# Another table of planner rules: which of sixteen rule sets orders each stretch of a two-layer transformer kernel

## The chip, the cores and the metric

The kernel runs on one core of one Trainium2 chip. The engines are TensorE (PE, with its weight loads as PEld), VectorE (DVE), ScalarE (ACT), GpSimd (POOL) and SyncE (SP, which issues the DMAs). The metric is the device time of one execution in microseconds, less being better. Each time is a median over several executions.

## The reference

Two attention blocks and two MLP blocks alternate over 2048 tokens of width 512, each behind a layer norm without weights and each with a residual. Both layers use the same weights. The attention has 32 heads of 16 columns; the MLP has 1792 hidden columns and a tanh GELU.

```python
def _A_ref(x, wqkv, wo):
    qkv = (x @ wqkv).reshape(B, S, 3, H, Dh)          # S = 2048, H = 32, Dh = 16
    q, k, v = ...                                     # each (B, H, S, Dh)
    scores = jnp.einsum("bhqd,bhkd->bhqk", q, k) * (Dh ** -0.5)
    p = _softmax(scores, axis=-1)
    o = jnp.einsum("bhqk,bhkd->bhqd", p, v)
    return o.transpose(0, 2, 1, 3).reshape(B, S, D) @ wo

def _B_ref(x, w1, b1, w2, b2):
    return _gelu(x @ w1 + b1) @ w2 + b2               # 512 -> 1792 -> 512

x = A_x
x = x + _A_ref(_layernorm(x), A_wqkv, A_wo)
x = x + _B_ref(_layernorm(x), B_w1, B_b1, B_w2, B_b2)
x = x + _A_ref(_layernorm(x), A_wqkv, A_wo)
return x + _B_ref(_layernorm(x), B_w1, B_b1, B_w2, B_b2)
```

All inputs are bfloat16. `B_x` isn't used.

## The kernel before, in words

**The work.** The unit of attention is a cell: one key tile of 128 keys, one group `a` of 32 of the 128 partitions (two heads), and 512 columns, which are 256 or 512 queries of those heads. There are 4096 cells over both layers. For each cell PE computes scores into one PSUM bank (`score`, L1444), an engine takes the exponential out of the bank, and PE multiplies the result with 17 columns of V, the 17th being ones for the softmax's sum (`pvs`, L2009). The banks: ACT's two slots hold banks 0, 1 and 3, 4 (`SLOTS`), with banks 2 and 5 lendable as a third to either slot (`THIRD`); bank 6 collects the products with V (`PVB`); bank 7 and, at times, 5 serve the projections and the MLP (`MISC`).

**Two ways to an exp.** ACT takes two or three cells with one instruction (`exps`, L1943), 128x1024 or 128x1536. DVE takes one cell with one instruction (`dfirst`, L1625), which writes a 16-bit integer that, read as bfloat16, is an approximate exponential; POOL adds constants to such a row three times over for shifted copies (`dchain`, L1717), and PE multiplies the four copies of a cell with V and three weighted copies of V (`VC`), so that a DVE cell has four matmuls with V where an ACT cell has one. Only the cells of five of the sixteen key tiles of each layer (`KD`, L54) may go to DVE. What of these DVE has not taken when ACT's own list for a head group is empty, ACT takes (`next_act`).

**Beside the attention** go, tile by tile: layer norms (`ln`, DVE, with a transposing DMA), the projections to Q, K, V (`proj`), the output projection (`wo`), the MLP's two halves (`hpair`, L1140, and `ytile`, L1192) and the GELU on ACT, two instructions of 128x3584 for 512 tokens (`gelu`, L1188). Quads of matmuls on 32-column strips carry them (L646). Weights stream from HBM through five buffers (`wload`, L1108).

**What sets the order.** Nothing is ordered by hand. While the program is built, a planner (`_Sched`) simulates the five engines: every activity above is a generator that yields operations with an estimated cost, and `run` (L438) takes again and again the operation that could start first, by priority. The order in which operations are taken becomes each engine's instruction order, and the semaphore waits follow from it. A clock per engine is part of that simulation; "planned time" below means it. The chip has no part in the choice: the order is frozen once the program is built.

**The rules.** Twelve of the planner's constants (`KNOBS`, L95) come in sixteen sets (`ORDERS`). At each step `tune` (L431) divides ACT's planned clock by 24 us (`STRETCH`) and looks in `PICKS` (L115) which set holds there. A set has, in this order:

- `PE`: how long after a matmul its result counts as visible to others (`LATENCY["pe"]`), 0.2175 to 0.2215 us.
- `SWAP`, `DCELL` (L1557): a DVE cell rides along with ACT's scores on bank 2 or 5 only if DVE's planned clock, with `DCELL` for each cell already riding, is no more than `SWAP` past the score's start.
- `EXT` (L1522), the same, 99, in all sets.
- `DULOW` (L1981, L2000): at how low a stock of rows for DVE's exps a half-filled round of products with V goes out.
- `SEVAC` (L333): the priority of DVE's other evacuations of PSUM; the one of DVE's exps is 0.4.
- `TOL` (L1559): how much later than the score's start a bank may come free for a riding DVE cell.
- `PTURG`, `PTLOW` (L1984, L1992): at how few free buffers for ACT's results the products with V become urgent, and ACT's results go first.
- `ALONE` (L1636): how far ACT's planned clock must lie past PE's before a DVE cell gets a score matmul of its own.
- `TAIL`, `OPENING` (L1464): how many cells a head group must have left for DVE to be given one.

Sets differ from set 0 in one or two of these, and by little. The first lines of the table and the function that reads it:

```python
KNOBS = ("PE", "SWAP", "EXT", "DULOW", "SEVAC", "TOL", "PTURG", "PTLOW", "DCELL", "ALONE", "TAIL", "OPENING")
ORDERS = (
    (0.219, 0.55, 99, 2, 0.2, 0.2, 6, 5, 0.68, 3.5, 10, 18),
    ...
def tune(self):
    k = min(int(self.clock["act"] // STRETCH), len(PICKS) - 1)
    if k != self.stretch:
        self.stretch = k
        globals().update(zip(KNOBS, ORDERS[PICKS[k]]))
        LATENCY["pe"] = PE
```

Against set 0: 1 and 2 have `PE` 0.2175 and 0.2215; 3 and 4 `SWAP` 0.7 and 0.45; 5 and 6 `SEVAC` 0.5 and 0.35; 7 `TOL` 0.1; 8 `ALONE` 2.5; 9 `TAIL` 8; 10 `OPENING` 22; 11 `PTLOW` 4; 12 `SWAP` 0.45 with `DCELL` 0.6; 13 `PTURG` 5; 14 `DULOW` 1 with `PTLOW` 3; 15 `PE` 0.2205 with `SWAP` 0.6.

Of the kernel before, what the change touches and what calls it, by code (L numbers as in the profile page):

```python
# [112 lines left out]
)  # L113
STRETCH = 24
PICKS = (1, 13, 4, 5, 13, 0, 1, 2, 3, 3, 11, 13, 13, 1, 3, 14, 1, 0, 13, 13, 13, 11, 3, 1, 14, 13,  # L115
         13, 0, 13, 12, 13, 1, 13, 13, 13, 1, 2, 1, 3, 4, 1, 2, 13, 13, 14, 9, 13, 13, 1, 3, 1, 1,
         13, 13, 0, 13, 1, 1, 1, 13)
LOG2E = 1.4426950408889634
E_SCALE = 0.25 * LOG2E * 128
E_BIAS = 15992.765054484162  # L120
# [145 lines left out]
class _Sched:  # L266
# [1854 lines left out]
```

## Time and profile before

| | us |
|---|---|
| median of 3 runs | 1427.75 (1427.6 to 1428.46) |
| the profiled execution | 1427.85 |
| its span, from the first to the last instruction | 1426.0 |
| busy in the span: PE / ACT / DVE / POOL | 1383.0 / 1399.0 / 1212.5 / 1012.1 |

The granted TensorE clock of the profiled execution is 1.000 in the mean. "Busy" sums the time in which an engine has an instruction under way; a matmul's record includes time in the pipeline, so PE's share is not a share of its peak. ACT's neighbouring records overlap: an instruction's mean duration is longer than the distance from one start to the next, which is the pitch at which ACT works through its queue. A group of instructions is given by its line; where a helper issues for several users (L646 for all quads), the tile's name tells them apart. An exp of DVE writes into several tensors whose space is lent for the purpose (`du`, `kt`, `v`), and so stands in several groups; ACT's likewise (`pt`, `q`, `v`, `g`, `kt`).

### The profile page before, as it was taken

Reading aid. Unit: us, or ns where it says so; the run is one execution under the profiler, and the core shown is the slowest. Engines: PE = TensorE matmul, PEld = TensorE weight load, DVE = VectorE, ACT = ScalarE, POOL = GpSimd, SP = SyncE. Lnnn points to the kernel's source line nnn. Section 1 sums busy time; section 2 is a strip of 40 time slices with the busy share of each in tenths; the row PEclk is TensorE's granted clock in tenths of the full one; section 3 lists DMA queues with packets and bytes.
Section 4 is the critical chain, followed back from the end, with each engine's and each line's share of the span. In section 5 each row is a group of like instructions: output and inputs, shape, how many; then the busy total and the mean of one; then the engine's idle time right before and its main releaser. Section 6 shows DMA issues by size and latency. Waiting matters only on the chain.

```text
span 1426.0 us, 45959 instructions
## 1 busy us (share of the span) xinstructions
PE 1383.0 (97%) x19370; PEld 421.3 (30%) x19370; DVE 1212.5 (85%) x2298; ACT 1399.0 (98%) x1404; POOL 1012.1 (71%) x1335
## 2 busy tenths in 40 slices
PE   8999999999999999999999999989999999999998
PEld 3222222222222222222222222222222222334345
DVE  7798999878898788997988868899979987999693
ACT  7999999999999999999999999999999999999995
POOL 1096998967787677886757757766866977877671
PEclk9999999999999999999999999999999999999999
DMA  6100001153111531213421153102163106411622
GB/s 177 44 2 1 2 2 33 39 156 107 50 46 39 142 113 30 53 31 107 124 82 40 45 156 105 39 1 46 31 183 90 34 24 182 131 39 33 205 66 69
DMA packets 145192, 103.51 MB, mean 73 GB/s; under 512 B 37085, under 2 KB 143965, under 8 KB 144989
## 3 DMA queue, kind: packets, MB, share of 16 engines
q1 hardware_dynamic: 144988, 100.57, 24.9%
q8 instruction: 156, 2.56, 0.8%
q14 instruction: 48, 0.39, 0.1%
HBM read 88.74 MB, written 4.19 MB: 65 GB/s over the span
## 4 chain that ended last, share of the span: by engine, by line
ACT 78%; PE 14%; DVE 6%; issue 1%; POOL 1%; DMA 0%; ACTq 0%; POOLq 0%
ACT pt L1943 57%; PE ps L646 6%; ACT q L1943 5%; PE ps L1444 4%; PE ps L2009 4%; ACT g L1943 4%; ACT kt L1943 4%; ACT v L1943 3%; ACT g L1188 3%; DVE du L1625 3%; ACT L1943 1%; ACT L1188 1%; POOL du L1717 0%; DVE ott L1021 0%; DVE stats L791 0%
## 5 line engine op out<-in xcount | busy, mean ns | idle before, releaser
L1943 ACT ACTIVATE pt<-ps 128x1024 bf16<-128x1024 f32 (+1 forms) x1061 | 1062.9, 1163 | 2.2 <-PE ps L1444 2.0
L1717 POOL INT64_ADD du<-du x981 | 759.9, 784 | 323.0 <-DVE du L1625 174.6
L1625 DVE TENSOR_SCALAR du<-ps 128x512 uint16<-128x512 f32 x1101 | 727.3, 683 | 127.2 <-PE ps L1444 118.4
L1444 PE MATMUL ps<-qp,kt 32*128 32x512 bf16 x4096 | 538.7, 384 | 21.4 <-ACT pt L1943 13.0
L2009 PE MATMUL ps<-du,vc 128*17 128x512 bf16 (+1 forms) x3351 | 361.1, 359 | 2.8 <-POOL du L1717 1.5
L1444 PEld LDWEIGHTS ps<-qp,kt 32*128 32x128 bf16 x4096 | 144.6, 91 | 573.5 <-ACT pt L1943 164.1
L2009 PE MATMUL ps<-pt,v 128*17 128x512 bf16 (+1 forms) x2549 | 268.3, 359 | 3.8 <-ACT pt L1943 2.4
L2009 PE MATMUL ps<-du,v 128*17 128x512 bf16 (+1 forms) x1228 | 171.0, 359 | 4.7 <-DVE xt L1012 2.1
L646 PE MATMUL ps<-xf,wr 128*32 128x512 bf16 (+1 forms) x2272 | 161.8, 371 | 0.2
L2009 PEld LDWEIGHTS ps<-du,vc 128*17 128x17 bf16 x3351 | 93.9, 89 | 94.9 <-issue 45.1
L646 PE MATMUL ps<-wr,g 128*32 128x512 bf16 x1504 | 110.6, 383 | 1.4 <-ACT g L1188 1.3
L2009 PE MATMUL ps<-kt,vc 128*17 128x512 bf16 (+1 forms) x533 | 101.0, 340 | 0.0
L1717 POOL INT64_ADD kt<-du x108 | 89.9, 836 | 14.1 <-DVE qp L1392 2.3
L1943 ACT ACTIVATE q<-ps 128x1024 bf16<-128x1024 f32 (+1 forms) x85 | 89.1, 1123 | 0.1
L2009 PEld LDWEIGHTS ps<-pt,v 128*17 128x17 bf16 x2549 | 66.3, 88 | 73.8 <-issue 51.4
L1167 DVE TENSOR_SCALAR g<-ps,hb1t 128x512 bf16<-128x512 f32 (+1 forms) x112 | 79.1, 706 | 8.7 <-PE ps L646 8.5
L1943 ACT ACTIVATE v<-ps 128x1024 bf16<-128x1024 f32 (+1 forms) x69 | 74.0, 1139 | 0.5
L1943 ACT ACTIVATE g<-ps 128x1024 bf16<-128x1024 f32 (+1 forms) x71 | 73.7, 1157 | 0.0
L1625 DVE TENSOR_SCALAR kt<-ps 128x512 uint16<-128x512 f32 x96 | 64.2, 682 | 6.6 <-PE ps L1444 6.3
L1943 ACT ACTIVATE kt<-ps 128x1024 bf16<-128x1024 f32 (+1 forms) x59 | 67.0, 1142 | 1.4
L1717 POOL INT64_ADD du<-kt x71 | 52.3, 740 | 11.4 <-DVE qp L1392 2.6
L646 PEld LDWEIGHTS ps<-xf,wr 128*32 128x32 bf16 x2272 | 40.5, 95 | 58.8 <-issue 46.4
(111 smaller groups left out, 1279.7 us busy)
## 6 DMA issues: line engine op xcount, KB each, us to landing
wr<-in_B_w_dram SPq DMA_DIRECT2D x243, 256.0 KB, 3.1
wr<-in_A_wqkv_dram SPq DMA_DIRECT2D x24, 256.0 KB, 2.8
wr<-in_A_wo_dram SPq DMA_DIRECT2D x17, 256.0 KB, 3.0
x<-in_A_x_dram SPq DMA_DIRECT2D x7, 512.0 KB, 4.3
pt<-in_B_w_dram SPq DMA_DIRECT2D x13, 256.0 KB, 3.3
kept<-x SPq DMA_DIRECT2D x4, 512.0 KB, 3.0
x<-kept SPq DMA_DIRECT2D x4, 512.0 KB, 3.9
out_dram<-x SPq DMA_DIRECT2D x16, 128.0 KB, 3.1
```

Source lines behind the costliest of these rows:

```text
L646: return [lambda e, a=a: e.matmul(out[32 * a:32 * a + 32, :], lhsT=lhsT[:, 32 * a:32 * a + 32], rhs=rhs, start=start, stop=stop, tile_posi ...
L1167: yield _Op("dve", 0.21 + n / 966, lambda e, fc=fc, pb=pb: e.tensor_scalar(T["G"][:, fc, q], pb, T["HB1T"][:, fc:fc + 1], None, op0=ALU.ad ...
L1188: lambda e, g=g: e.activation(out=g, in_=g, func=ACT.Gelu_apprx_tanh), reads=gk, writes=gk, prio=2)
L1444: return (lambda e: e.matmul(o, lhsT=lhsT, rhs=rhs, start=True, stop=True, tile_position=(32 * a, 0)), ["K%d.%d.%d" % (l, gb, kt // 4), "Q ...
L1625: yield _Op("dve", 0.682, lambda e: e.tensor_scalar(u, self.bank(b), E_SCALE, E_BIAS, op0=ALU.mult, op1=ALU.add), reads=["B.%d" % b], writ ...
L1717: add = lambda out, src, k: lambda e: e.int64_add(out.bitcast(I64), src.bitcast(I64), k * SHIFT * ONES)
L1943: yield _Op("act", 0.052 + 0.4267 * n, lambda e, src=src, dst=dst: e.activation(out=dst, in_=src, func=ACT.Exp, scale=0.25), reads=["B.%d" ...
L2009: op.fns.append(lambda e, o=o, lhsT=q[0][0][m], rhs=q[0][1][:, n * m:n * m + n], a=a, st=st, sp=sp: e.matmul(o, lhsT=lhsT, rhs=rhs, start= ...
```

## The change

Only the table `PICKS` is another one. Its 60 entries were found by a search that goes through the stretches in order of time, tries the sets on each, replays the engines over the plans that come out, keeps the six plans that have come furthest two stretches on, and goes to the next stretch. The search is not part of the kernel; the table is its result. 53 of the 60 entries differ.

```diff
@@ -112,9 +112,9 @@
 STRETCH = 24
-PICKS = (1, 13, 4, 5, 13, 0, 1, 2, 3, 3, 11, 13, 13, 1, 3, 14, 1, 0, 13, 13, 13, 11, 3, 1, 14, 13,
-         13, 0, 13, 12, 13, 1, 13, 13, 13, 1, 2, 1, 3, 4, 1, 2, 13, 13, 14, 9, 13, 13, 1, 3, 1, 1,
-         13, 13, 0, 13, 1, 1, 1, 13)
+PICKS = (0, 3, 12, 5, 9, 7, 7, 7, 10, 10, 5, 3, 12, 5, 14, 12, 4, 1, 5, 8, 13, 5, 4, 13, 12, 2, 8,
+         4, 13, 12, 15, 10, 11, 8, 12, 7, 15, 4, 1, 7, 1, 14, 8, 7, 7, 15, 3, 13, 13, 12, 3, 5, 1,
+         8, 13, 13, 3, 0, 13, 5)
```

The sets themselves, the planner, the activities and all constants outside the table are the same. How often each set is used: before, set 13 in 22 stretches, 1 in 15, 3 in 6, 0 in 4, 2 and 14 in 3 each, 4 and 11 in 2, 5, 9 and 12 in 1, and 6, 7, 8, 10 and 15 in none; after, 13 in 8, 5, 7 and 12 in 7 each, 3 and 8 in 5, 1 and 4 in 4, 10 and 15 in 3, 0 and 14 in 2, 2, 9 and 11 in 1, and 6 in none. Since an operation taken earlier or later in one stretch changes what is ready in the next, the order differs from the first differing stretch on, in stretches with equal entries too.

## The prediction, made before the change was run

> **What bounds the kernel now.** I read the page's first two parts, then busy time by stretch of the run, then the groups of instructions by line, the waits, and last the chain that ended last with the timeline of its end. The page (busy time, share and count of each engine; granted clock in tenths, 40 slices):
>
> ```profile
> span 1426.0 us, 45959 instructions
> PE 1383.0 (97%) x19370; PEld 421.3 (30%) x19370; DVE 1212.5 (85%) x2298; ACT 1399.0 (98%) x1404; POOL 1012.1 (71%) x1335
> PEclk9999999999999999999999999999999999999999
> ```
>
> The busy time by window, cut where the queue of exps starts to be full and where the last exp ends (columns: stretch, its length, busy time and count of PE, PEld, DVE, ACT, POOL, clock, DMA):
>
> ```profile
> 0.00:24.00 24.00, 19.74 (x329) 8.32 (x329) 18.54 (x72) 15.82 (x20) 4.01 (x17) 1.00 0.68 199
> 24.00:1400.08 1376.08, 1340.92 (x18541) 398.80 (x18533) 1183.63 (x2202) 1372.05 (x1368) 1006.98 (x1316) 1.00 0.25 71
> 1400.08:1426.00 25.92, 22.29 (x508) 14.16 (x508) 10.33 (x25) 11.16 (x18) 1.15 (x2) 1.00 0.07 23
> ```
>
> The reader is to see that ACT is idle 24 - 15.82 = 8.18 us at the start, 1376.08 - 1372.05 = 4.03 us in the whole middle, and 25.92 - 11.16 = 14.76 us at the end. So the span is ACT's busy time plus 27. PE's 97% is a weaker statement, as the waits (engine, line, who is waited for: total, times, longest) show:
>
> ```profile
> PEld ps L1444 <- ACT pt L1943: 164.1, 380, 1.7
> PEld ps L1444 <- DVE du L1625: 114.0, 256, 0.9
> ACT pt L1943 <- PE ps L1444: 2.0, 5, 0.7
> POOL du L1717 <- DVE du L1625: 174.6, 81, 53.9
> ```
>
> PE's score matmuls (L1444) wait 164.1 us for exps to free a bank; ACT waits 2.0 us for scores. The queue ahead of ACT is full, and what sets the time is how much work ACT is given.
>
> That work is fixed but for one thing. Of the 4096 score cells (one key tile, one row group, 512 queries), each is exponentiated by ACT, two or three to an instruction (L1943), or by DVE (L1625) with POOL multiples (L1717). The rows, by form for ACT's largest tile, and DVE's by tile:
>
> ```profile
> L1943 ACT ACTIVATE pt<-ps 128x1024 bf16<-128x1024 f32 x903 | 862.4, 1097 | 1.4 <-PE ps L1444 1.3
> L1943 ACT ACTIVATE pt<-ps 128x1536 bf16<-128x1536 f32 x158 | 228.6, 1537 | 0.8 <-PE ps L1444 0.7
> L1444 PE MATMUL ps<-qp,kt 32*128 32x512 bf16 x4096 | 538.7, 384 | 21.4 <-ACT pt L1943 13.0 <-ACT kt L1943 2.7 <-DVE du L1625 0.7
> L1625 DVE TENSOR_SCALAR du<-ps x1101: 624/683/695, 66.9 to 1392.2; 128x512 uint16<-128x512 f32 x184
> L1625 DVE TENSOR_SCALAR kt<-ps x96: 630/683/693, 212.4 to 1381.8; 128x512 uint16<-128x512 f32 x96
> L1625 DVE TENSOR_SCALAR v<-ps x20: 653/681/693, 344.1 to 1314.5; 128x512 uint16<-128x512 f32 x20
> ```
>
> DVE takes 1101 + 96 + 20 = 1217 cells, ACT 4096 - 1217 = 2879. The code allows DVE five key tiles of sixteen, 1280 cells, so 63 allowed cells now fall to ACT.
>
> **The change, part by part.** It exchanges the 60 numbers that say which of sixteen sets of planner constants holds in each 24 us of planned time. 53 of them differ. No instruction's shape, tile or count changes by itself; five queues (PE, ACT, DVE, POOL, and SP with its loads and transposes) come out in another order from the first stretch on. So the terms are those that an order can move.
>
> First, cells between ACT and DVE. What a cell costs ACT is its pitch, since the records overlap; pieces of the chain (start, length, what) and two neighbours of the timeline give it:
>
> ```profile
> 1015.41 9.17 ACT pt L1943 x10
> 26.82 1.65 ACT L1943 ACTIVATE kt<-ps 128x1536 bf16<-128x1536 f32 x1
> 28.15 8.01 ACT L1943 ACTIVATE pt<-ps 128x1024 bf16<-128x1024 f32 x7
> ```
>
> A pair is 9.17 / 10 = 0.917 us, a triple 28.15 - 26.82 = 1.33 us; a cell out of pairs is 0.458 us. How many cells an order can move is not in a trace of one order, so I bound it by how unevenly DVE gets cells now. DVE's exps by window, cut at the gelus (stretch, length, busy, count in brackets):
>
> ```profile
> 293.65:462.94 169.29, 98.75 (x149) 1.00 0.28 81
> 462.94:655.45 192.51, 121.14 (x182) 1.00 0.26 71
> 655.45:819.24 163.79, 89.29 (x135) 1.00 0.30 83
> 819.24:1036.89 217.65, 121.51 (x183) 1.00 0.23 63
> 1036.89:1161.62 124.73, 77.23 (x117) 1.00 0.32 93
> 1161.62:1314.28 152.66, 95.54 (x146) 1.00 0.31 90
> 1314.28:1400.08 85.80, 43.95 (x67) 1.00 0.46 135
> ```
>
> That is 979 cells in 1106.4 us, 0.885 per us; the stretches run from 0.78 to 0.956. If the two poor ones from 655 to 1037 (0.824 and 0.841) rise to the mean, DVE gains (0.885 - 0.824) x 163.8 + (0.885 - 0.841) x 217.7 = 20 cells, 9.2 us off ACT. If the two rich ones (0.945 from 463, 0.956 from 1162) fall to it, it loses 0.060 x 192.5 + 0.071 x 152.7 = 22 cells, 10.1 us on ACT. All 63 would be 28.9 us. I take +12 cells, a little over half the gain, -5.5 us. Why a gain: the trace leaves room for it on all who would pay, and the selection looks at progress, which is cells while ACT is full. Who pays for 12: DVE 12 x 0.683 = 8.2 us out of 1426.0 - 1212.5 = 213.5 idle; POOL the adds of six row pairs, with the medians of these rows
>
> ```profile
> L1717 POOL INT64_ADD du<-du x981: 395/612/1044, 68.9 to 1393.7; - x197
> L1717 POOL INT64_ADD kt<-du x108: 609/1037/1042, 168.8 to 1382.1; - x108
> ```
>
> 6 x (0.612 + 1.037) = 9.9 us out of 414 idle; PE three more value matmuls per cell, of which four start within 0.21 us:
>
> ```profile
> 922.24 0.38 PE L2009 MATMUL ps<-pt,v 128*17 128x512 bf16 x2
> 922.45 0.38 PE L2009 MATMUL ps<-pt,v 128*17 128x512 bf16 x2
> ```
>
> 12 x 3 / 4 x 0.21 = 1.9 us under the 164.1 us that PE waits for ACT. Without that cover PE's 1.9 us would come back whole.
>
> Second, ACT's waits for scores. They are 2.0 us in 5 waits and can fall to nothing (-2.0). Upwards, if one PE wait of the longest kind, 1.7 us, got through to ACT in each of the eight stretches between gelus, +13.6. The row of the same planner is the nearest, so I take a quarter of it more, +0.5: PE is early hundreds of times and late five.
>
> Third, pairs and triples. Three pairs become two triples for 3 x 0.917 - 2 x 1.33 = 0.09 us; ten such exchanges either way are 0.9 us. I take 0, since no row favours a sign.
>
> Fourth, the start: the first rule differs only in the planner's PE latency, 0.2175 against 0.219, and no DVE exp starts before 66.9 us. I take 0 and 0.6 us either way from the largest ACT wait on the evacuations there (0.65 us, below). Fifth, the end, where little is left to plan: the last exp has ended and these pieces of the chain follow.
>
> ```profile
> 11.69 0.58 ACT L924 CAST q<-ps 128x512 bf16<-128x512 f32 x1 [0.65 <-DVE qp L918]
> 1402.73 5.79 PE ps L646 x104
> 1410.85 12.37 PE ps L646 x336
> 1423.23 0.69 DVE x L1219
> ```
>
> I take 0, with one late evacuation, 0.7 us, either way. Sixth, SP's loads move with their users; the weights' matmuls wait 0.2 us for DMA in the whole run,
>
> ```profile
> L646 PEld LDWEIGHTS ps<-wr,g 128*32 128x32 bf16 x1504 | 26.7, 95 | 43.6 <-issue 35.2 <-DMA wr<-in_B_w_dram 0.2
> ```
>
> hidden behind PE's own queue (issue), so nothing; uncovered, a load issued late is a PE wait and lies in the second term.
>
> Sum: -5.5 + 0.5 = -5.0 us. The profiled execution took 1427.85 us for its span of 1426.0, 1.85 around it, and lies 0.1 above the median of 1427.75. The span becomes 1421.0, the execution 1422.85, the median 1422.7, which is 0.35% faster. A measurement of this kernel can tell about 0.2%, 2.9 us, or 2.9 / 0.458 = 6 cells, from no change.
>
> The clock is one thing on which a page bears. Every slice of the clock row is 9, and fill-in matmuls (L1432) stand where PE would be quiet; the opening shows what a slow one is (min/median/max in ns):
>
> ```profile
> L1432 PE MATMUL ps<-vc x236: 378/379/392, 75.9 to 1401.6; 128*32 128x512 bf16 x118
> L1432 PE MATMUL ps<-du,ident x13: 379/634/634, 2.3 to 6.7; 128*128 128x512 bf16 x13
> ```
>
> An order that left PE a gap would cost 634 - 379 = 255 ns per matmul until the clock was back; at one start per 0.21 us some 16 starts in 3.4 us, 4 us a gap. The Trainium skill, TensorE: Matmul & The Clock Gate, Part 1, says that a quiet window of about 3.4 us halves the clock; by it the new order pays only for gaps that long, and the longest PE wait above is 1.7 us, so by that rule too the sum keeps a zero here.
>
> **The rivals.** *DVE loses cells* (slower). In the new list the rules that make taking a cell for DVE harder are commoner: set 7 (a bank must be free 0.1 us after the score's planned start, not 0.2) 7 times against none, sets 4 and 12 (DVE's planned lag below 0.45 us, not 0.55) 11 against 3. For the forecast speak sets 3 (lag 0.7) 5 against 6 and 8 (lone cells sooner) 5 against none. If the rich stretches fall to the mean, the bound above: 22 cells, +10.1, 1437.9; from 6 cells on it is slower. At two thirds, 15 cells, +6.9, 1434.6.
>
> *ACT starves* (slower). One wait of 1.7 us per stretch between gelus, because a queue ordered for a replay runs up against one late release: +13.6, and with the 12 cells gained +8.1, 1435.8. Against it: 2.0 us now, and two banks' worth of exps ahead of ACT. It decides from 5.5 + 2.9 = 8.4 us of new ACT waits.
>
> *The order hardly matters* (no change). Fewer than 6 cells move net, waits stay: 1427.7, 1424.9 to 1430.6. For it: ACT's middle is already full to 4.03 us in 1376.
>
> *DVE and POOL get in each other's way* (slower). POOL adds now wait for the query copies and DVE's copies stretch:
>
> ```profile
> POOL du L1717 <- DVE qp L1392: 19.1, 43, 3.5
> L1392 DVE TENSOR_SCALAR qp<-q,mask x91: 267/345/1155, 13.4 to 1339.7; 128x512 bf16<-128x512 bf16 x75, 128x256 bf16<-128x256 bf16 x16
> ```
>
> If all 91 copies took the longest time, DVE would lose 91 x 0.81 = 74 us, and at 0.683 a cell, with a tenth not found in its 213.5 idle, 11 cells, +5.0, 1432.7. The Trainium skill, SBUF — State Buffer, Who interferes with whom, has it that a DVE instruction in a two-port mode and a GpSimd instruction exclude each other for the whole of the first; the copies' spread from 345 to 1155 ns agrees. Against it: the planner holds the two apart (held_off), and neither engine is the bound.
>
> **How the numbers follow.** Forecast, more cells on DVE: 0.43. Loses cells: 0.22. Starves: 0.13. Hardly matters: 0.17. Port: 0.05. So faster 0.43, same 0.17, slower 0.22 + 0.13 + 0.05 = 0.40. The forecast's own range is 1413 (half of the 63 cells, 14.4 us) to 1424.9. The whole range reaches from 1412 (1413 and half of ACT's 2.0 us of waits) to 1438, the bound of the lost cells; what is left out is a plan in which two of these meet, or one that moves more than half of the 63.
>
> **What would show it.** Right: L1625 counts about 1229 over its tiles, L1943 holds 12 cells fewer, ACT's busy time is near 1393.5 and its idle time from 24 us to the last exp near 4.5; PE's wait for exps stays above 100 us; the poor stretches from 655 to 1037 gain most; the clock row stays all 9. Wrong in the first term: L1625 below 1217 and ACT's busy time above 1399. Wrong in the second: a wait of ACT for L1444 well over 2.0 us. Wrong in the fifth: more than 25.9 us from the last exp to the end. What would make the forecast wrong is above all a replay whose progress was ahead in DVE's queue, not in exps that ACT is spared.

## The result and the profile after

The changed kernel takes 1418.41 us (1417.62 to 1419.86, 6 runs) against 1427.86 us before (6 runs): a ratio of 0.9935, 95% interval 0.9922 to 0.9947, so 9.45 us or 0.65% faster. The profiled execution took 1417.91 us for a span of 1416.1.

The page of the changed kernel, first two parts:

```profile
span 1416.1 us, 45896 instructions
PE 1376.4 (97%) x19314; PEld 418.2 (30%) x19314; DVE 1215.3 (86%) x2319; ACT 1389.3 (98%) x1398; POOL 1030.9 (73%) x1371
PEclk9999999999999999999999999999999999999999
```

ACT's busy time fell from 1399.0 to 1389.3 us, 9.7, and the span by 9.9. The same three stretches as before, cut again at 24 us and at the end of the last exp (stretch, length, then busy time and count of PE, PEld, DVE, ACT, POOL):

```profile
0.00:24.00 24.00, 20.19 (x335) 8.39 (x339) 18.87 (x73) 16.50 (x21) 4.01 (x17) 1.00 0.69 201
24.00:1389.98 1365.98, 1334.07 (x18479) 395.72 (x18471) 1185.86 (x2222) 1361.65 (x1361) 1025.70 (x1352) 1.00 0.25 72
1389.98:1416.10 26.12, 22.11 (x512) 14.11 (x504) 10.53 (x26) 11.16 (x18) 1.15 (x2) 1.00 0.07 23
```

ACT is idle 7.50 us at the start (8.18 before), 4.33 in the middle (4.03) and 14.96 at the end (14.76): 26.8 us in all against 27.0. The gain is work that ACT no longer has, and no idle time. DVE's exps, as counted by line in the changed kernel, say which work:

```profile
L1625 DVE TENSOR_SCALAR du<-ps x1130: 624/681/892, 66.2 to 1376.5; 128x512 uint16<-128x512 f32 x189
L1625 DVE TENSOR_SCALAR kt<-ps x95: 625/680/692, 150.9 to 1356.1; 128x512 uint16<-128x512 f32 x95
L1625 DVE TENSOR_SCALAR v<-ps x13: 646/687/692, 361.1 to 1263.7; 128x512 uint16<-128x512 f32 x13
```

1130 + 95 + 13 = 1238 cells, 21 more than the 1217 before; 21 x 0.458 = 9.6 us. They came mostly where the old order was poor, as the same count by window shows, first before, then after:

```profile
24.00:720.00 696.00, 411.39 (x625) 1.00 0.22 60
720.00:960.00 240.00, 129.34 (x195) 1.00 0.25 70
960.00:1400.08 440.08, 262.99 (x397) 1.00 0.32 90
```

```profile
24.00:720.00 696.00, 415.03 (x632) 1.00 0.22 62
720.00:960.00 240.00, 144.61 (x219) 1.00 0.22 64
960.00:1389.98 429.98, 255.16 (x388) 1.00 0.31 91
```

From 720 to 960 us DVE takes 24 cells more; up to 720 it takes 7 more, and from 960 its rate is unchanged (0.902 per us, both). (The second three counts add up to 1239, as an exp across a cut stands in both stretches.) The three further matmuls with V per cell, 63 in all, cost PE nothing. These are the matmuls with zeros that fill up rounds (L2017) and those that only keep PE going (L1432), before and then after:

```profile
L2017 PE MATMUL ps<-vc,zero 128*17 128x512 bf16 x245 | 51.3, 381 | 0.0
L1432 PE MATMUL ps<-vc 128*32 128x512 bf16 x236 | 18.5, 383 | 0.0
L1432 PE MATMUL ps<-vc,zero 128*17 128x512 bf16 x64 | 5.6, 384 | 0.0
```

```profile
L2017 PE MATMUL ps<-vc,zero 128*17 128x512 bf16 x182 | 41.8, 381 | 0.0
L1432 PE MATMUL ps<-vc 128*32 128x512 bf16 x200 | 15.7, 384 | 0.2 <-DVE du L1625 0.2
L1432 PE MATMUL ps<-vc,zero 128*17 128x512 bf16 x44 | 4.0, 384 | 0.0
```

Rounds hold 63 zero matmuls fewer, exactly as many as the new cells bring, and the keep-warm ones fell by 56. PE's busy time went down by 6.6 us.

### The profile page after: what moved, and what is told of

Its sections match the earlier page's. It is cut to its first block, busy times and chain, and to the rows that moved or that the text cites. A ratio compares the mean times of both kernels' runs of the same rounds, so it can differ in the third digit from the quotient of the medians.

```text
span 1416.1 us, 45896 instructions
## 1 busy us (share of the span) xinstructions
PE 1376.4 (97%) x19314; PEld 418.2 (30%) x19314; DVE 1215.3 (86%) x2319; ACT 1389.3 (98%) x1398; POOL 1030.9 (73%) x1371
## 4 chain that ended last, share of the span: by engine, by line
ACT 71%; PE 18%; DVE 8%; DMA 1%; issue 1%; POOL 1%; SPq 0%; ACTq 0%; POOLq 0%; DVEq 0%
ACT pt L1943 52%; PE ps L646 7%; PE ps L1444 6%; PE ps L2009 6%; ACT g L1943 5%; DVE du L1625 4%; ACT q L1943 4%; ACT v L1943 4%; ACT g L1188 3%; ACT kt L1943 2%; DMA xf<-pt 1%; ACT L1943 1%; ACT L1188 1%; DMA b1c<-in_B_b_dram 0%; POOL du L1717 0%
## 5 line engine op out<-in xcount | busy, mean ns | idle before, releaser
L1943 ACT ACTIVATE pt<-ps 128x1024 bf16<-128x1024 f32 (+1 forms) x1048 | 1047.1, 1163 | 2.2 <-PE ps L1444 1.9
L1717 POOL INT64_ADD du<-du x1027 | 786.6, 776 | 298.5 <-DVE du L1625 143.6
L1625 DVE TENSOR_SCALAR du<-ps 128x512 uint16<-128x512 f32 x1130 | 744.4, 682 | 120.4 <-PE ps L1444 111.0
L1444 PE MATMUL ps<-qp,kt 32*128 32x512 bf16 x4096 | 539.3, 384 | 20.1 <-ACT pt L1943 10.7
L2009 PE MATMUL ps<-du,vc 128*17 128x512 bf16 (+1 forms) x3449 | 372.3, 358 | 1.3 <-POOL kt L1717 0.7
L1444 PEld LDWEIGHTS ps<-qp,kt 32*128 32x128 bf16 x4096 | 144.0, 91 | 575.5 <-ACT pt L1943 159.7
L2009 PE MATMUL ps<-pt,v 128*17 128x512 bf16 (+1 forms) x2508 | 266.7, 358 | 4.1 <-ACT pt L1943 2.5
L2009 PE MATMUL ps<-du,v 128*17 128x512 bf16 (+1 forms) x1266 | 176.6, 358 | 2.9 <-DVE xt L1012 0.8
L646 PE MATMUL ps<-xf,wr 128*32 128x512 bf16 (+1 forms) x2272 | 162.2, 371 | 1.2 <-DMA xf<-pt 0.9
L2009 PEld LDWEIGHTS ps<-du,vc 128*17 128x17 bf16 x3449 | 98.7, 89 | 89.6 <-issue 43.2
L646 PE MATMUL ps<-wr,g 128*32 128x512 bf16 x1504 | 110.2, 383 | 0.6 <-ACT g L1188 0.6
L1717 POOL INT64_ADD kt<-du x111 | 92.8, 839 | 16.7 <-DVE pt L840 3.8
L2009 PE MATMUL ps<-kt,vc 128*17 128x512 bf16 (+1 forms) x519 | 103.3, 342 | 0.4 <-POOL kt L1717 0.4
L1943 ACT ACTIVATE g<-ps 128x1024 bf16<-128x1024 f32 (+1 forms) x89 | 90.1, 1122 | 0.0
L2009 PEld LDWEIGHTS ps<-pt,v 128*17 128x17 bf16 x2508 | 64.4, 88 | 72.3 <-issue 51.2
L1943 ACT ACTIVATE q<-ps 128x1024 bf16<-128x1024 f32 (+1 forms) x78 | 83.0, 1137 | 0.2 <-PE ps L2009 0.2
L1943 ACT ACTIVATE v<-ps 128x1024 bf16<-128x1024 f32 (+1 forms) x69 | 76.6, 1163 | 0.5
L1717 POOL INT64_ADD du<-kt x83 | 56.7, 689 | 12.1 <-DVE ott L1021 6.5
L1943 ACT ACTIVATE kt<-ps 128x1024 bf16<-128x1024 f32 (+1 forms) x55 | 63.8, 1186 | 0.9
L2009 PEld LDWEIGHTS ps<-du,v 128*17 128x17 bf16 x1266 | 45.9, 89 | 44.2 <-issue 13.8
```

Of the source, the lines that this page charges most:

```text
L646: return [lambda e, a=a: e.matmul(out[32 * a:32 * a + 32, :], lhsT=lhsT[:, 32 * a:32 * a + 32], rhs=rhs, start=start, stop=stop, tile_posi ...
L1444: return (lambda e: e.matmul(o, lhsT=lhsT, rhs=rhs, start=True, stop=True, tile_position=(32 * a, 0)), ["K%d.%d.%d" % (l, gb, kt // 4), "Q ...
L1625: yield _Op("dve", 0.682, lambda e: e.tensor_scalar(u, self.bank(b), E_SCALE, E_BIAS, op0=ALU.mult, op1=ALU.add), reads=["B.%d" % b], writ ...
L1717: add = lambda out, src, k: lambda e: e.int64_add(out.bitcast(I64), src.bitcast(I64), k * SHIFT * ONES)
L1943: yield _Op("act", 0.052 + 0.4267 * n, lambda e, src=src, dst=dst: e.activation(out=dst, in_=src, func=ACT.Exp, scale=0.25), reads=["B.%d" ...
L2009: op.fns.append(lambda e, o=o, lhsT=q[0][0][m], rhs=q[0][1][:, n * m:n * m + n], a=a, st=st, sp=sp: e.matmul(o, lhsT=lhsT, rhs=rhs, start= ...
```

## The experiments

Each run was compared with the kernel before on the same chip; where a run is set against the changed kernel, it is by what each differs from the kernel before. The "in-step theory" of some of the expectations (ACT and PE are both full and go in step, so that relief of one alone is not felt) arose from the runs with less work, further below. Two questions: do the cells on DVE set the time, and is ACT alone the bound?

**Other tables.** They are the same program with other entries in `PICKS`. First the new entries shuffled:

```diff
-PICKS = (0, 3, 12, 5, 9, 7, 7, 7, 10, 10, 5, 3, 12, 5, ...)
+PICKS = (13, 13, 10, 5, 13, 0, 12, 10, 8, 7, 13, 1, 15, 12, ...)
```

> The entries of the new table in a random order: each rule set holds in as many stretches as in the changed kernel, in other places. Counted in the built program, DVE gets 1212 cells (before 1217, changed kernel 1238). Theory (cells on DVE set the time at 0.458 us each): 5 cells fewer than before, 1430.2 us, ratio 1.0016. Rival (the mix of rules makes the gain, the loosened sets 3, 5 and 8): close to the changed kernel, 1418 to 1421.

Measured: 1435.65 us, ratio 1.0052 (1.0037 to 1.0067), 7.3 us slower. In this one random order the same mix of rules makes no gain, so their places matter. It is 5 us slower than the cells say.

The two tables spliced, the new one first:

```diff
-PICKS = <the 60 new entries>
+PICKS = <the first 30 new entries> + <the last 30 old ones>
```

> The new table's first 30 entries, then the old 30. Counted in the built program: 1229 cells on DVE, 12 more than before, and 192 keep-warm matmuls (before 236, changed kernel 200). Cells theory: 12 x 0.458 = 5.5 us less than before, 1422.5 us, ratio 0.9962. Rival (the gain lies in the places of the second half's rules): within 2 us of before. In-step theory: the same as the cells theory or somewhat better, as both counts fall.

Measured: 1424.44 us, ratio 0.9975 (0.9964 to 0.9986), 4.4 us faster. The cells theory holds to 1.1 us; ACT's idle time is 1.9 us longer than before. That this table would do somewhat better than its cells, as the in-step theory allowed, did not come: counting both kinds of keep-warm matmuls (L1432) it has 296, against 300 before and 244 in the changed kernel.

```diff
-PICKS = <the 60 new entries>
+PICKS = <the first 30 old entries> + <the last 30 new ones>
```

> The old table's first 30 entries, then the new table's last 30. Counted in the built program: 1212 cells on DVE, 5 fewer than before. If the new entries of the second half carry a gain of their own (the changed kernel is some 5 us ahead of the run with only the first half new): 1422 to 1424 us, ratio 0.996. If an entry is good only on the plan that leads up to it: no gain, by the cells 2.3 us slower, ratio 1.0016, and more where ACT waits, as in the shuffled table.

Measured: 1439.59 us, ratio 1.0078 (1.0061 to 1.0095), 10.8 us slower. The second half of the new table, which behind the new first half takes the run from 4.4 us ahead (half_new) to 9.45, ends 10.8 us behind when it follows the old first half. An entry is good on the plan that leads up to it.

```diff
-PICKS = <the 60 new entries>
+PICKS = <the first 10 new entries> + <the last 50 old ones>
```

> The new table's first 10 entries, then the old ones. Counted in the built program: 1220 cells on DVE, between the kernels; but PE issues 316 matmuls that only keep its clock up (L1432, four at a time), against 236 before and 200 in the changed kernel: the planner found more places where PE had nothing ready. Cells theory (1217 + 3, 0.458 us each): 1426.5 us, ratio 0.999. In-step theory (a place where PE has nothing ready is lost to ACT too): slower than before, 1432 or more, ratio above 1.003, with ACT waiting some 5 us more.

Measured: 1443.78 us, ratio 1.0107 (1.0091 to 1.0123), 15.0 us slower with 3 cells more on DVE. ACT's waits in that run (engine, line, who is waited for: total, times, longest) show it starving:

```profile
ACT pt L1941 <- PE ps L2007: 13.8, 5, 5.9
ACT pt L1941 <- PE ps L1442: 5.0, 5, 3.1
```

(L1941, L2007 and L1442 are L1943, L2009 and L1444 of the kernel before.) Before, the second wait was 2.0 us and the first absent: 16.8 us more, for 15.0 us of time and 1.3 us of work saved. The longest, on the timeline (start, length, tile, count, idle time before):

```profile
1355.70 1.53 ACT L1941 ACTIVATE pt<-ps 128x1536 bf16<-128x1536 f32 x1
1363.09 3.28 ACT L1941 ACTIVATE pt<-ps 128x1536 bf16<-128x1536 f32 x3 [5.86 <-PE ps L2007]
```

Here ACT's next exp stands behind a product with V on PE for 5.86 us. The in-step expectation had the sign, not the size.

One set throughout:

```diff
-PICKS = <the 60 new entries>
+PICKS = (3,) * 60
```

> Set 3 (a DVE cell may ride along with DVE 0.7 us behind, not 0.55) in all 60 stretches. Counted in the built program: 1188 cells on DVE, 29 fewer than before, in 1122 two-cell and 221 three-cell exps on ACT against 1156 and 189. My reading in the prediction (the looser lag gives DVE more cells, so that more of set 3 is faster): faster than before, ratio under 0.998. Cells theory: (1122 - 1156) x 0.904 + (221 - 189) x 1.33 = 11.8 us and one single exp of 0.44 more on ACT, 12.3 us, 1441 us, ratio 1.0086, and more if ACT waits more.

Measured: 1444.74 us, ratio 1.0112 (1.0097 to 1.0127), 16.0 us slower. More of set 3 is not faster: with it throughout, DVE gets 29 cells fewer. PE issues more scores alone; it has 1550 score groups instead of 1449, in the built program and in the trace. No table with set 0 throughout was run, so how much of the loss is the looser lag, and how much having one set everywhere, is open.

Taken together, with the work of ACT's exps at the commonest distance from start to start in the records, 0.904 us for two cells and 1.33 for three, the number of each counted in the built program, and ACT's idle time as span less busy time of the page:

| table | cells on DVE | ACT's exps of 2 / 3 cells | their work against before, us | ACT idle, us | time against before, us |
|---|---|---|---|---|---|
| before | 1217 | 1156 / 189 | 0 | 27.0 | 0 |
| changed | 1238 | 1159 / 180 | -9.3 | 26.8 | -9.45 |
| half_new | 1229 | 1153 / 187 | -5.4 | 28.9 | -4.4 |
| shuffled | 1212 | 1154 / 192 | +2.2 | 31.3 | +7.3 |
| old_then_new | 1212 | 1131 / 207, one single | +1.8 | 34.6 | +10.8 |
| new_then_old | 1220 | 1156 / 188 | -1.3 | 43.6 | +15.0 |
| one_rule_3 | 1188 | 1122 / 221, one single | +12.3 | 31.1 | +16.0 |

Work plus the change of idle time gives the time to within 1.5 us in each row. Busy and idle time add up to the span by definition, so what the table tests is that number and price of the exps account for ACT's busy time; that ACT is the cause it does not show by itself. Both terms are needed: in three of the five other tables the waits are the larger one.

PE's busy time moves with the time as well: in the order of the table by 0, -6.6, -5.8, +5.9, +9.0, +11.3 and +15.9 us. It is not a measure of PE's work alone, for it rises by 6.8 us in the next run, whose PE instructions are those of the changed kernel. But no run gave PE more work, so it is not excluded that the time follows PE upwards as it follows ACT.

**More work in the changed kernel, its order frozen.**

```diff
+            if n == 2 and u > 100 and u % 7 == 0:
+                fns = [lambda e, src=src[:, i, :], dst=dst[:, i, :]: e.activation(out=dst, in_=src, func=ACT.Exp, scale=0.25) for i in range(2)]
```

> The changed kernel, its order unchanged, with 158 of its two-cell exps on ACT done as two one-cell instructions; the result is the same. ACT's work grows by 158 instruction overheads; from the pitches 0.917 and 1.33 us for two and three cells an instruction's overhead is 0.917 - 2 x 0.413 = 0.09 us, so 14 us. Theory (ACT's work sets the time): all of it comes out, 1432 us, about 1% above the changed kernel, ratio to before 1.003. Rival (PE or the banks set the time and ACT has slack): the time stays at 1418 to 1421, ratio 0.993 to 0.995.

Measured: 1428.12 us, ratio to the kernel before 0.9996 (0.9987 to 1.0006). That is 0.2 us less than before where the changed kernel has 9.45 less, so 9.3 us above the changed kernel. ACT's busy time rose by 9.6, from 1389.3 us:

```profile
PE 1383.2 (97%) x19314; PEld 420.6 (30%) x19314; DVE 1216.6 (85%) x2319; ACT 1398.9 (98%) x1556; POOL 1033.4 (72%) x1371
```

The time lies between theory and rival, because the overhead was priced too high: it is 9.3 / 158 = 0.06 us, not 0.09. The two halves of a split exp start 0.478 us apart in the median, so that together they take 0.05 us more than the 0.904 of one exp. What was added on ACT comes out whole.

```diff
+        cols = (slice(0, 256), slice(256, 512)) if self.firsts % 8 == 0 else (slice(0, 512),)
+        yield _Op("dve", 0.682, [lambda e, c=c: e.tensor_scalar(u[:, c], self.bank(b)[:, c], E_SCALE, E_BIAS, ...) for c in cols],
```

> The changed kernel, its order unchanged, with 154 of its 1238 exps on DVE done as two instructions of 256 columns each; the result is the same. DVE's work grows by 154 overheads of some 0.15 us (0.683 us for 512 columns, at 0.96 columns a ns 0.53 of it for the columns), 23 us. Theory (DVE's 200 us of idle time pay for it): less than 4 us, ratio to before under 0.9965. Rival (DVE is nearly a bound by now, since PE's scores wait 127 us for DVE to free banks): over half of the 23 us come out, ratio above 1.0015.

Measured: 1421.42 us, ratio 0.9949 (0.9934 to 0.9964), 6.9 us less than before and so 2.6 us above the changed kernel, whose interval (0.9922 to 0.9947) overlaps this one. DVE's busy time rose by 7.0 us to 1222.3, not by 23: the two halves together last 0.748 us in the median, 0.07 more than a whole one (0.680), which makes some 10 us in all. So most of DVE's added work stays hidden; whether a small part comes out is not clear of the noise.

**Less work in the kernel before, its order frozen.** This is the other direction, and here the theory met trouble.

```diff
+            if n == 2 and u > 100 and u % 50 == 0:
+                src, dst = src[:, 0:1, :], dst[:, 0:1, :]
```

> The kernel before, its order unchanged, with 21 of its two-cell exps on ACT (evenly spread after the first hundred) cut to one cell, so that 21 cells' exps are left out: ACT gets the relief that 21 more cells on DVE would give, and DVE, POOL and PE get no more work. Theory (the time is ACT's work plus fixed gaps): 21 x 0.43 = 9.0 us less, ratio 0.9937, 1418.8 us. Rival (the gain came from the new order itself, fewer stalls on PE or DVE): under 2 us, ratio above 0.9985.

Measured: 1426.92 us, ratio 0.9989 (0.9980 to 0.9999): 1.4 us less, not 9, which is what the rival said. The records tell half of why. From the start of a one-cell exp to the start of the next passes 0.49 to 0.92 us (median 0.81), though in the run with split exps the two halves start 0.48 us apart. With two slots in turn, the scores of the other slot aren't there sooner: in 20 of the 21 places the next exp starts within 0.03 us of the end of the scores that it reads.

So the same relief without short exps:

```diff
+            if n == 3 and self.threes % 9 == 0:
+                src, dst = src[:, 0:2, :], dst[:, 0:2, :]
```

> The kernel before, its order unchanged, with 21 of its 189 three-cell exps on ACT cut to two cells, so that 21 cells' exps are left out as in the run with 21 two-cell exps cut to one, but no exp becomes shorter than 0.90 us. In that run the 21 one-cell exps were followed only 0.68 to 0.87 us later by the next, not 0.44: the next slot's scores were not there yet. Theory (ACT's work sets the time as long as an exp lasts longer than the other slot's turnaround): 21 x (1.33 - 0.904) = 8.9 us less, ratio 0.9938. Rival (ACT and PE in step, so that relief of ACT alone is never felt): as with the two-cell exps, 1 to 3 us less, ratio 0.998 or more.

Measured: 1425.61 us, ratio 0.9976 (0.9966 to 0.9985): 3.1 us of 8.9. Just above the rival's range and far from the theory. The timeline around one cut shows where the rest goes, first before, then with the cut (L1946 is L1943 there; the count is of neighbours merged into one row):

```profile
1276.39 2.99 ACT L1943 ACTIVATE v<-ps 128x1536 bf16<-128x1536 f32 x2
1279.28 5.33 ACT L1943 ACTIVATE pt<-ps 128x1024 bf16<-128x1024 f32 x5
```

```profile
1274.18 2.56 ACT L1946 ACTIVATE v<-ps 128x1536 bf16<-128x1536 f32 x2
1276.64 1.02 ACT L1946 ACTIVATE pt<-ps 128x1024 bf16<-128x1024 f32 x1
1278.20 4.20 ACT L1946 ACTIVATE pt<-ps 128x1024 bf16<-128x1024 f32 x4 [0.54 <-PE ps L1444]
```

The exp after the cut starts 1276.64 - 1274.18 = 2.46 us behind the first shown, 0.43 less than before (2.89). The one after that waits 0.54 us for PE's scores, where no wait was, and the lead is gone. In the mean of 19 cuts the lead (by how much an exp starts earlier than before, counted from the cut) is 0.38 us at the next exp and 0.16 three exps on.

Relief of PE alone:

```diff
+                self.skip = getattr(self, "skip", 0) + 2
...
+                            if skip:
+                                op.fns.append(None)
+                                continue
```

> The kernel before, its order unchanged, with 42 rounds of products with V left out on PE (184 matmuls, 42 x 0.21 = 9.0 us), two near each of the 21 places of the run with less work on ACT; ACT keeps all its work. Theory now (ACT and PE are both full and go in step, a score group for an exp, so that relief of one of them is not felt): under 3 us less, ratio above 0.998. Rival (PE alone sets the time, since relief of ACT alone gave 1.4 us): most of the 9 us, ratio 0.9945 or less. The first theory, ACT alone: 0.

Measured: 1429.12 us, ratio 1.0004 (0.9994 to 1.0013): nothing, though PE's busy time fell by 4.5 us, from 1383.0 to 1378.5. PE alone isn't the bound, for all its 97%. In the frozen order relief of ACT alone gave little too, so this run alone doesn't tell the two engines apart.

Both together, first with the one-cell exps:

```diff
+            if n == 2 and u > 100 and u % 50 == 0:
+                self.skip = getattr(self, "skip", 0) + 2
+                src, dst = src[:, 0:1, :], dst[:, 0:1, :]
```

> Both edits at once: 21 cells' exps left out on ACT (9.0 us) and 42 rounds of products with V left out on PE (9.0 us) near the same 21 places, the order that of the kernel before. Theory (ACT and PE in step): clearly more than the sum of the two alone, 4 to 9 us less, ratio 0.994 to 0.997. Rival (the frozen order's other waits, on DVE and POOL, hold the time, and only a new order moves it): about the sum of the two alone, ratio above 0.998.

Measured: 1425.63 us, ratio 0.9977 (0.9967 to 0.9986), 3.2 us less: more than the two alone (1.4 and nothing), though the intervals of this run and of the one with less work on ACT overlap; below the 4 expected, with the short exps' own cost in it.

Then with the three-cell exps:

```diff
+            if n == 3 and self.threes % 9 == 0:
+                self.skip = getattr(self, "skip", 0) + 2
+                src, dst = src[:, 0:2, :], dst[:, 0:2, :]
```

> The kernel before, its order unchanged, with 21 three-cell exps on ACT cut to two cells (8.9 us, alone worth 3.1 us) and, right behind each, up to two rounds of products with V left out on PE (41 rounds, 41 x 0.21 = 8.7 us; such rounds alone were worth nothing). In the run with the cut alone, ACT's lead of 0.43 us after a cut was gone after one to three exps, because the scores of the following exps came when they had come before. Theory (ACT and PE go in step, and an order fixes how much PE does between two exps): 5 to 9 us less, ratio 0.9937 to 0.9965. Rival (DVE's and POOL's steps hold the frozen order just as much): as with the cut alone, about 3 us, ratio 0.997 or more.

Measured: 1423.75 us, ratio 0.9965 (0.9952 to 0.9978), 5.1 us less, at the lower edge of the in-step theory and above the rival: 3.1 from ACT alone, nothing from PE alone, 5.1 from both at the same places. The intervals of the two runs (0.9966 to 0.9985 and 0.9952 to 0.9978) overlap, so the 2 us between them are not shown by the times alone; the leads point the same way. In the mean of 19 cuts the lead now stays longer, 0.40 us at the next exp and 0.30 three exps on (0.38 and 0.16 with the cut alone). Of the 8.9 us some 3.8 don't come out: ten exps on, the mean lead is down to 0.25 us. At the first three cuts no round of the required kind stood right behind, and PE's relief came 4 to 15 exps later; the rest I can't place. That DVE's or POOL's fixed steps hold it is not shown.

So the theory now: work added on ACT comes out whole. Work taken off ACT in a frozen order comes out by a third, and by rather more if PE's work between the same exps shrinks too. The changed kernel got 9.45 us for 9.3 us less work, the frozen kernel 3.1 for 8.9. That the new order gets all of it because PE has less to do at the right places too fits these runs and the 56 matmuls fewer on PE, but no run shows it place by place.

None of the tables run was faster than the changed kernel's.

## Why the prediction was right, and where it was off

*What bounds.* Right that ACT's work is the time: the run with more work on ACT shows it upwards, and 9.7 us less busy time with the idle time unchanged is what the changed kernel shows. Downwards it holds for the new order and not for the old one with less work in it. Wrong was the reading of the 164.1 us that "PE's score matmuls" wait for exps. That row is PEld's, the weight loads, which stand ready early while PE is still at the matmuls before: in 157.8 of the 164.1 us PE has a matmul under way. At the score groups with such a wait PE's last start before and first start after lie 0.312 us apart in the median, at the other score groups 0.312 too. PE's own wait is another row; both rows, before and then after:

```profile
PEld ps L1444 <- ACT pt L1943: 164.1, 380, 1.7
PE ps L1444 <- ACT pt L1943: 13.0, 30, 1.4
```

```profile
PEld ps L1444 <- ACT pt L1943: 159.7, 369, 0.9
PE ps L1444 <- ACT pt L1943: 10.7, 33, 0.6
```

So PE had 13 us of such cover, not 164, and between two exps mostly none; the frozen orders fit that. The sign "PE's wait for exps stays above 100 us" came true (159.7) and says nothing about PE's slack. The 1.9 us of PE's price were still nothing, for another reason than the one given: the matmuls took columns that had held zeros.

*First term, cells.* The mechanism and, nearly, the price per cell were right (0.458 us taken, 9.3 / 21 = 0.44 found), the number was mis-sized: 12 cells (-5.5 us) against 21 measured (-9.3 us of exps). The 12 was a choice of a little over half of the 20 that the poor stretches had to give, and no row fixed it. The search got all of it in the place named: from 655 to 1037 us DVE takes 24 cells more (0.89 per us, 0.83 before), nearly all of the rise between 720 and 960. That a gain rather than a loss would come was argued from the selection alone; three of the five other tables have fewer cells than before. The bound of 63 cells stayed far off: 42 are still left to ACT.

*Second term, waits.* +0.5 us against 0.1 less in this row of the changed kernel (2.0 before), and 0.3 more idle time in the whole middle:

```profile
ACT pt L1943 <- PE ps L1444: 1.9, 4, 1.0
```

The size was right, but the base was too small, and its reason, that PE is early hundreds of times, was the misread PEld row; that nothing came of it is in part luck. Counted from start to start, ACT's exps before take 23.9 us more in all than at their commonest distances (0.904 and 1.33 us), and 15.0 of these fall at 287 places where the next exp starts just behind the end of an operation of PE. Most of that lies under overlapping records and so in no wait row. In the changed kernel it is 24.1 and 16.7 us: hardly changed, as forecast.

*Third to sixth.* Triples fell by 9 and pairs rose by 3, which is the 21 cells themselves. The start gained 0.7 us of idle time, just over the bound given (0.6), the end lost 0.2, within its bound. The weights' loads stayed hidden (0.2 us, both); matmuls of L646 wait 0.9 us for a transpose (`xf`), where they waited for none before.

*The rivals.* That the rules which make taking a cell harder would lose cells did not come true: the new table has more of sets 4, 7 and 12, and 21 cells more. The counts of sets don't tell: set 3, which loosens, gives DVE the fewest cells of all tables tried when it holds throughout, and the shuffled table has the same counts of sets and none of the gain. (Set 3 was listed for the forecast with 5 stretches against 6, but that is fewer.) The stricter sets were not run by themselves. That ACT starves is real, with 16.8 us of new waits in one spliced table, but not in this one. The port: the query copies on DVE have a median of 343 ns after, 345 before, and a longest of 944 after, 1155 before, so a new order did not make them collide more. With the rule of the Trainium skill named there (SBUF — State Buffer, Who interferes with whom) the traces agree: the slowest copy of the kernel before, 1155 ns, has POOL's instructions under way in 1010 of them, and its next two, 1053 and 948 ns, in 906 and 801, which leaves 145 to 147 ns for each. The clock row is all 9, and the clock rule of the Trainium skill named in the prediction (TensorE: Matmul & The Clock Gate, Part 1) stayed without effect, as forecast.

*The profile's busy share.* The Trainium skill, Perfetto Trace Analysis, DVE / Act Engine Instruction, says that a record of ACT ends when the last write is acknowledged. The trace agrees in that records overlap: two-cell exps of the kernel before last 1097 ns in the mean and start 904 ns apart when they follow directly; what fills the rest of a record no run here shows. So a gap of under some 0.19 us between two exps is not seen in a busy time. In the run with 21 three-cell exps cut, 8.9 us of work left but ACT's busy time fell by only 5.8 us, from 1399.0:

```profile
PE 1381.6 (97%) x19370; PEld 421.2 (30%) x19370; DVE 1211.8 (85%) x2298; ACT 1393.2 (98%) x1404; POOL 1012.1 (71%) x1335
```

Counted from start to start, as above, its exps take 29.7 us over their commonest distances where it was 23.9: of the 8.9 us, 5.8 went into such gaps, and 3.1 are left, as much as the medians differ.

## What to carry to other kernels

When two engines pass work to and fro through a few buffers and both are full, take work off one and look whether the other's stream has room at the same place; here a price per unit from one engine held for more work at once and for less work only in a new plan. Read a wait of PEld as a weight load that is early, and PE's own rows for PE's slack. A table of choices found in order of time is one object: its parts, spliced behind another beginning, were worth +10.8 and +15.0 us here, and its entries in another order +7.3.

## What was not expected of the hardware

An exp of one bank between exps of the other slot did not let the next one start after 0.48 us, the distance of one-cell exps back to back, but after 0.81 us in the median of 21: in this order the other slot's scores were not done earlier. And leaving out 184 of PE's matmuls, 9.0 us by the estimate of 0.21 us a round and 4.5 us of PE's busy time, moved a kernel whose PE shows 97% busy by nothing (ratio 1.0004, 0.9994 to 1.0013).
